# Emptying an attention accumulator at a chunk's end: one ACT copy of its first half, the sum on GpSimd, its second half at the end of the step

## The chip, the cores and the metric

The kernel runs on one core of one Trainium2 chip. The metric is the device time of one execution in microseconds (us). A core has a matrix engine (TensorE: PE, with its weight loads listed as PEld), a vector engine (VectorE, DVE), a scalar engine (ScalarE, ACT), GpSimd (POOL) and SyncE (SP), which here only issues DMAs. Each engine works through its own instructions in order.

## What is computed

```python
scores = (1 / S) * z @ z.T                 # per batch, B = 4, S = 3008, 64 columns of z
attn   = maximum(scores, 0) ** 2
x      = u * (attn @ v)                    # v: 3008 x 256
out    = (sigmoid(x @ w_gate) * (x @ w_val)) @ w_out     # 256 -> 1536 -> 256, 12032 tokens
```

Everything is float32. The kernel keeps precision by splitting operands into a high part and a rest and adding three products.

## The kernel before

**Two stages.** The attention runs for the first half of the time, the gated network (products of 7 per block, L635 to L734) for the second. The change lies in the attention.

**Chunks and steps.** Queries are cut into 6 chunks of 512 (the last 448) per batch, so 24 chunks in all, here numbered 0 to 23. A chunk takes 12 steps, one for each pair of 128-key tiles; `steps` lists all 288, and `k = g % 12` is a step's place in its chunk. Scores are symmetric, so many steps take a tile that an earlier chunk computed, turned and stored in DRAM (`back(s)` is true): they are read back by SP (`load_back`, five steps ahead) and need no scores. Steps of chunk 0 of each batch compute everything, those of chunk 5 nearly nothing.

**One turn of the loop (L854).** For step g the engines get, in this order: PE the scores of step g+2 (`pe_scores`, L354, 6 matmuls); at a chunk's end `keep`; SP the stores of turned tiles; DVE the turning of step g+1 (`turn`, L429 and L433); ACT for step g+2 ReLU and square (`square`, L363 and L364) and rounding to the high part (`round_up`, L379, or DVE's L377); DVE the rest `al` (`rest`, L384); then a list of side work (preparing z, v and the network's weights); last PE the 24 matmuls of step g (`pe_pv`, L507). These are 12 for each half d of the 256 columns of v, and each of the 12 takes 64 of the 128 rows, so that two run side by side into two banks: an accumulator is a pair of banks whose two parts must be added.

**Banks.** PSUM has 8 banks. Banks 0 and 1 take scores. The other six are three pairs that rotate (`pair_of_banks`, L329): `acc_of(b, c, d)` uses pair (2C + d) mod 3 for chunk C. So the new chunk's d = 0 uses the pair that was free, and its d = 1 uses the pair that held d = 0 of the chunk before. The third pair, which held d = 1, takes the scores of every odd step (`scores_of`).

**A chunk's end.** In the loop's turn k = 0 of the next chunk, `keep(..., False)` (L514) does for d = 0 and then d = 1: an ACT copy of one bank to SBUF (L527) and a DVE sum of the other bank to it (L528):

```python
for d in range(NB):
    to, acc = by_half(t[:, d, 0:n]), acc_of(b, c, d)
    nc.scalar.activation(to, product(acc[:, 0, 0:n]), AF.Copy)
    nc.vector.tensor_tensor(to, product(acc[:, 1, 0:n]), to, op=ALU.add)
```

PE's matmuls of d = 1 in that turn write the pair of d = 0 and wait for both. The place `t` lies in the area `keep_a`, two halves in turns; the same area holds tiles that came as stored and are still to be turned (`as_stored`, L455, read by `turn_late`, L482) in batch 0. In the turn k = 1 `keep(..., True)` lets SP store the sums to DRAM (L523). GpSimd only issues DMAs in the attention.

Of the kernel before, what the change touches and what calls it, by code (L numbers as in the profile page):

```python
# [13 lines left out]
AF = mybir.ActivationFunctionType  # L14
ALU = mybir.AluOpType
# [11 lines left out]
def kernel(  # L27
# [10 lines left out]
    nc = tc.nc  # L38
    P = 128
    B, S, D = u.shape  # L40
# [3 lines left out]
    CH = 512  # L44
    NCH = (S + CH - 1) // CH
    NPAIR = (S + 255) // 256
    NB = D // P
# [6 lines left out]
    def chunk(c):  # L54
        return min(CH, S - c * CH)
# [10 lines left out]
    def area(tag, name=None):  # L66
        return pool.tile([P, sizes[tag] * KB], F32, tag=tag, name=name or tag)

    v_a, z_a, zq_a, r_a, ah_a, al_a, al2_a, turned_a, raw_a, zt_a, keep_a, w_a, spare_a = map(area, sizes)
# [3 lines left out]
    def second(tag, name):  # L73

        if tag not in later:
            later[tag] = area(tag, name)
        return later[tag]
# [3 lines left out]
    def part(a, kb, cols, dt=F32):  # L81

        ap = a[:, int(kb * KB) : int(kb * KB) + cols]
        return ap if dt is F32 else ap.bitcast(dt)
# [8 lines left out]
    def product(ap):  # L93

        return ap.rearrange("p (n t) -> p t n", t=2)

    def products(ap):
        return ap.rearrange("p j (n t) -> p j t n", t=2)

    def by_half(ap):  # L100
        return ap.rearrange("p (t n) -> p t n", t=2)

    def by_halves(ap):
        return ap.rearrange("p j (t n) -> p j t n", t=2)
# [19 lines left out]
    def order(b, c):  # L124
        mirrored = [i for i in range(2 * c) if shared(b, i // 2, c)]
        own = [i for i in range(NPAIR) if i not in mirrored]
        last = []
        if halved(b, c):
            own.remove(2 * c + 1)
            last = [2 * c + 1]  # L130
        if not mirrored:
            return own + last
        own.sort(key=lambda i: (i // 2 > c, i // 2 < c and c < NCH - 1, i))
        m = len(own) + len(mirrored)
        places = [x * m // len(own) for x in range(len(own))]
        if (b, c) == (B - 1, NCH - 1):
            places = list(range(len(own)))
        line = [None] * m
        for x, i in zip(places, own):
            line[x] = i  # L140
        rest = iter(mirrored)
        return [next(rest) if i is None else i for i in line] + last

    steps = [(b, c, i) for b in range(B) for c in range(NCH) for i in order(b, c)]
# [96 lines left out]
    def z_place(b, p):  # L241
        n = (b * NCH + p) % 7
        return part(z_a, 2 * n, CH, F32R), part(z_a, 14 + 2 * n, CH, F32R)
# [14 lines left out]
    def turn_z(b, p):  # L258
        z_t[b, p] = part(zt_a, 2 * (p % 2), CH)
        nc.vector.transpose(out=z_t[b, p], in_=z_raw.pop((b, p)))  # L260

    def z_high(b, p):
        nc.scalar.activation(z_place(b, p)[0], z_t[b, p], AF.Copy)  # L263

    def z_low(b, p):
        hi, lo = z_place(b, p)
        nc.vector.tensor_tensor(lo, z_t[b, p], f32(hi), op=ALU.subtract)
# [61 lines left out]
    def pair_of_banks(n):  # L329

        k = 2 + 2 * (n % 3)
        return banks[:, k : k + 2]

    def scores_of(s):

        g = number[s] - 2
        if g % 2:
            return pair_of_banks(2 * (max(g, 0) // NPAIR) + 2)
        return banks[:, 0:2]

# [143 lines left out]
    def acc_of(b, c, d):  # L484

        return pair_of_banks(2 * (b * NCH + c) + d)

    def pe_pv(s):

        b, c, i = s  # L490
        n, k = chunk(c), number[s] % NPAIR
        (ah, al), (vh, vl) = a_of(s), v_place(b, i)
        whole = number[s] >= len(steps) - 2
        for d in range(NB):
            acc = acc_of(b, c, d)
            ds = slice(d * P, (d + 1) * P)
            for j in range(2):
                passes = [(vh, ah), (vl, ah), (vh, al)]
                if i == NPAIR - 1 and j == 1:
                    del passes[1]  # L500
                for x, (vx, ax) in enumerate(passes):
                    start = k == 0 and j == 0 and x == 0
                    ends = j == 1 and x == len(passes) - 1
                    halves = [(0, slice(0, P))] if whole else [(r, rows_half(r)) for r in range(2)]
                    for r, p in halves:
                        stop = ends and number[s] in ((len(steps) - 1, len(steps) - 3)[r], number[s] - k + NPAIR - 1)
                        nc.tensor.matmul(acc[:, r, 0:n], vx[p, j, ds], moving(ax[p, j, 0:n]), start=start, stop=stop)  # L507
                yield
# [2 lines left out]

    sums = dram.tile([P, NB, N], F32, name="sums")

    def keep(b, c, store):  # L514
        n, t0 = chunk(c), b * S + c * CH
        C = b * NCH + c
        if C == B * NCH - 1:
            t = part(turned_a, 8, 2 * CH)
        else:
            t = part(keep_a, 4 * ((C + 1) % 2) if b < B - 1 else 0, 2 * CH)  # L520
        t = t.rearrange("p (h q) -> p h q", h=NB)
        if store:
            nc.sync.dma_start(sums[:, :, t0 : t0 + n], t[:, :, 0:n])  # L523
            return
        for d in range(NB):
            to, acc = by_half(t[:, d, 0:n]), acc_of(b, c, d)
            nc.scalar.activation(to, product(acc[:, 0, 0:n]), AF.Copy)  # L527
            nc.vector.tensor_tensor(to, product(acc[:, 1, 0:n]), to, op=ALU.add)  # L528

# [3 lines left out]
    B1, B2, T12, T34 = range(4)  # L535

    def operand(G, i):

        if G % 2 == 0:
            places = (z_a, 8 * i), (zq_a, 0) if i == T34 else (z_a, 8 * i + 4)  # L540
        else:
            a, o = (v_a, 48 + 8 * i) if i < 2 else (second("r", "x"), 8 * (i - 2))
            places = (a, o), (a, o + 4)
        return [part(a, o, 2 * CH, F32R).rearrange("p (i q) -> p i q", i=2) for a, o in places]
# [201 lines left out]
    with tc.manual_schedule():  # L746
# [5 lines left out]
        def at(when, g, f, *args):  # L752
            when.setdefault(g, []).append((f, args))

        def run(when, g):
            for f, args in when.get(g, ()):
                f(*args)

        per = NPAIR * NCH
        for b in range(1, B):  # L760
            g0 = (b - 1) * per
            for p in range(NCH):
                g = g0 + (3 * NPAIR + 4 * p if p < 3 else 4 * NPAIR + 4 * (p - 3) if p < 5 else 5 * NPAIR)
                if (b, p) == (1, 1):
                    g = 5 * NPAIR + 3
# [7 lines left out]
            for i in range(NPAIR):  # L773
                g = g0 + (2 * NPAIR + 4, 2 * NPAIR + 8, 3 * NPAIR + 2, 3 * NPAIR + 7)[i] if i < 4 else line[i - 4]
# [12 lines left out]
        g = 3 * per  # L787
# [10 lines left out]
        g = len(steps) - NPAIR  # L798
# [55 lines left out]
        for g, (b, c, i) in enumerate(steps[:-2]):  # L854
            nxt = steps[g + 2]
            k = g % NPAIR
            early = g < NPAIR
            if g < 3:
                for _ in pe_pv(steps[g]):
                    pass  # L860
            pe_scores(nxt)
            if early:
                if k + 2 < NPAIR:
                    v_low(0, k + 2)
                if k + 5 < NPAIR:
                    load_v(0, k + 5)
                if k in (2, 3, 5):
                    z_low(0, {2: 3, 3: 4, 5: 5}[k])
                if k in (0, 2, 4):
                    turn_z(0, k // 2 + 3)  # L870
            for s in steps[g + 5 : g + 8]:
                if number[s] - g == (7 if comes_late(s) else 5):
                    load_back(s)
            if k == 0 and g:
                keep(*steps[g - 1][:2], False)
            if k == 1 and g > 1:
                keep(*steps[g - 2][:2], True)
            store_turned(steps[g])
            turn(steps[g + 1])
            if not back(nxt):  # L880
                square(nxt)
            round_up(nxt)
            rest(nxt)
            if g + 4 < len(steps):
                turn_late(steps[g + 4])
            run(before, g)
            if early and k + 3 < NPAIR:
                v_high(0, k + 3)
            if early and k in (1, 2, 4):
                z_high(0, {1: 3, 2: 4, 4: 5}[k])  # L890
            run(after, g)
            if g >= 3:
                for _ in pe_pv(steps[g]):
                    pass
# [5 lines left out]
        extra = {}  # L900
        last = len(groups) * NF - 1
# [16 lines left out]
                    at(extra, (J + NF + (x > 0), (7, 1, 2, 3)[x]), finish, G - 1, t, h)  # L918
        at(extra, (0, -1), load_o, 0)
        at(extra, (0, 1), load_w, 2, 1)  # L920
        at(extra, (0, 7), keep, *steps[-1][:2], False)
        at(extra, (0, 7), keep, *steps[-1][:2], True)
        for F in range(1, NF):
            at(extra, (F - 1, 7), load_o, F)
        for x, F in enumerate((3, 4, 5)):
# [27 lines left out]
        for J in range(last + 1):  # L953
            run(extra, (J, -1))
            for value in range(2):
                k = 4 * value
# [92 lines left out]
```

## Time and profile before

| | |
|---|---|
| median of 3 runs | 1923.06 us (1919.26 to 1923.71) |
| the profiled execution | 1921.55 us, its span 1919.5 us |
| PE busy over the span | 97% |
| DVE, ACT, POOL busy | 81%, 59%, 48% |
| mean granted clock of TensorE | 0.994 |

The span is the time between the first and the last instruction of the profiled execution; 2.05 us lie around it. PE's share is high throughout, so time is won only where PE stands still or runs at a lower clock.

### The profile page before, as it was taken

Reading aid. Unit: us, or ns where it says so; the run is one execution under the profiler, and the core shown is the slowest. Engines: PE = TensorE matmul, PEld = TensorE weight load, DVE = VectorE, ACT = ScalarE, POOL = GpSimd, SP = SyncE. Lnnn points to the kernel's source line nnn. Section 1 sums busy time; section 2 is a strip of 40 time slices with the busy share of each in tenths; the row PEclk is TensorE's granted clock in tenths of the full one; section 3 lists DMA queues with packets and bytes.
Section 4 is the critical chain, followed back from the end, with each engine's and each line's share of the span. In section 5 each row is a group of like instructions: output and inputs, shape, how many; then the busy total and the mean of one; then the engine's idle time right before and its main releaser. Section 6 shows DMA issues by size and latency. Waiting matters only on the chain.

```text
span 1919.5 us, 33838 instructions
## 1 busy us (share of the span) xinstructions
PE 1868.9 (97%) x12614; PEld 1638.3 (85%) x12614; DVE 1563.3 (81%) x2004; ACT 1140.3 (59%) x1520; POOL 921.4 (48%) x853
## 2 busy tenths in 40 slices
PE   9999999999998999999999999999999999999998
PEld 7878988879877888889888888888888888888898
DVE  7887688887888787776888797978888797878886
ACT  8876788767877678765444444444444444534443
POOL 4323200231013200000777777867777777878775
PEclk9999999999999999999999999999999999999999
DMA  7778677986789878886633425242433425242431
GB/s 198 186 197 224 175 177 203 254 262 199 171 220 260 277 174 210 192 234 221 221 92 96 126 69 134 89 102 83 119 100 100 114 69 143 80 102 82 108 100 37
DMA packets 548645, 297.43 MB, mean 155 GB/s; under 512 B 489344, under 2 KB 506176, under 8 KB 548480
## 3 DMA queue, kind: packets, MB, share of 16 engines
q1 hardware_dynamic: 531248, 248.48, 49.2%
q0 software_dynamic: 14832, 46.38, 7.8%
q8 instruction: 99, 1.62, 0.4%
q10 hardware_dynamic: 2400, 0.41, 0.1%
q14 instruction: 66, 0.54, 0.1%
HBM read 192.02 MB, written 103.15 MB: 154 GB/s over the span
## 4 chain that ended last, share of the span: by engine, by line
PE 70%; DVE 2%; ACT 2%; issue 1%; DMA 1%; SPq 0%; DVEq 0%; POOL 0%; POOLq 0%
PE banks L703 18%; PE banks L507 15%; PE banks L643 11%; PE banks L644 11%; PE banks L645 11%; PE banks L354 2%; ACT ah L379 1%; ACT r L363 1%; ACT r L364 1%; PE banks L734 1%; DVE al L384 1%; DMA shared<-turned 1%; DVE keep L528 0%; DVE turned L433 0%; DVE spare L433 0%
## 5 line engine op out<-in xcount | busy, mean ns | idle before, releaser
L507 PE MATMUL banks<-ah,v 64*128 64x512 f32 (+1 forms) x4496 | 748.1, 376 | 39.2 <-DVE keep L528 31.4
L507 PEld LDWEIGHTS banks<-ah,v 64*128 64x128 f32 x4496 | 598.8, 188 | 98.2 <-DVE keep L528 38.8
L507 PE MATMUL banks<-al,v 64*128 64x512 f32 (+1 forms) x2296 | 621.4, 377 | 4.7 <-DVE al L384 3.6
L676 POOL TENSOR_TENSOR keep<-keep,spare 128x512 f32<-128x512 f32 (+1 forms) x284 | 387.3, 1374 | 240.2 <-DVE keep L668 239.1
L384 DVE TENSOR_TENSOR al<-r,ah 128x1024 fp32r<-128x1024 f32 (+1 forms) x287 | 341.2, 1191 | 163.0 <-ACT ah L379 154.9
L507 PEld LDWEIGHTS banks<-al,v 64*128 64x128 f32 x2296 | 387.9, 188 | 37.5 <-DVE al L384 11.0
L379 ACT ACTIVATE ah<-r 128x1024 fp32r<-128x1024 f32 (+1 forms) x252 | 257.5, 1035 | 50.9 <-PE banks L507 28.6
L680 ACT ACTIVATE h<-keep 128x512 fp32r<-128x512 f32 (+1 forms) x144 | 89.7, 623 | 283.7 <-POOL keep L676 280.5
L668 DVE TENSOR_TENSOR zt<-banks,zt 128x512 f32<-128x512 f32 (+1 forms) x288 | 193.8, 673 | 66.7 <-ACT zt L662 59.3
L363 ACT ACTIVATE r<-banks 128x1024 f32<-128x1024 f32 (+2 forms) x169 | 163.5, 967 | 124.4 <-PE banks L354 116.5
L686 POOL TENSOR_TENSOR h<-keep,h 128x512 fp32r<-128x512 f32 (+1 forms) x143 | 186.9, 1307 | 55.7 <-ACT h L680 55.7
L672 ACT ACTIVATE spare<-spare 128x512 f32<-128x512 f32 (+1 forms) x288 | 174.1, 618 | 65.2 <-DVE spare L668 63.6
L668 DVE TENSOR_TENSOR spare<-banks,zt 128x512 f32<-128x512 f32 (+1 forms) x288 | 188.3, 674 | 22.6 <-PE banks L645 22.6
L364 ACT ACTIVATE r<-r 128x1024 f32<-128x1024 f32 (+2 forms) x169 | 169.6, 1003 | 5.4
L662 ACT ACTIVATE zt<-banks 128x512 f32<-128x512 f32 (+1 forms) x144 | 84.0, 583 | 145.7 <-PE banks L645 141.5
L231 POOL DMA_DIRECT2D w_gv<-w x24 | 13.4, 560 | 324.5 <-ACT w L225 311.0
L354 PE MATMUL banks<-z 64*128 64x512 f32 (+2 forms) x1020 | 162.8, 370 | 0.0
L643 PE MATMUL banks<-z,v 128*128 128x512 f32 x378 | 144.1, 381 | 0.0
L645 PE MATMUL banks<-z,v 128*128 128x512 f32 x378 | 143.3, 379 | 0.0
L354 PEld LDWEIGHTS banks<-z 64*128 64x128 f32 x1020 | 126.5, 196 | 10.6 <-ACT z L263 0.8
L680 ACT ACTIVATE v<-keep 128x512 fp32r<-128x512 f32 (+1 forms) x144 | 89.0, 618 | 58.6 <-POOL keep L676 50.5
L668 DVE TENSOR_TENSOR keep<-banks,spare 128x512 f32<-128x512 f32 (+1 forms) x144 | 97.3, 676 | 32.2 <-PE banks L645 28.7
(157 smaller groups left out, 3606.9 us busy)
## 6 DMA issues: line engine op xcount, KB each, us to landing
v<-w_gv SPq DMA_DIRECT2D x75, 896.0 KB, 4.7
r<-shared SPq DMA_DIRECT2D x72, 512.0 KB, 4.6
shared<-turned SPq DMA_DIRECT2D x236, 128.0 KB, 2.8
r<-shared SPq DMA_DIRECT2D x38, 448.0 KB, 5.6
shared<-spare SPq DMA_DIRECT2D x128, 128.0 KB, 3.8
out_dram<-turned SPq DMA_DIRECT2D x176, 64.0 KB, 2.2
w_gv<-w POOLq DMA_DIRECT2D x24, 448.0 KB, 5.0
sums<-keep SPq DMA_DIRECT2D x20, 512.0 KB, 3.7
```

The lines of the kernel that those rows point to most:

```text
L354: nc.tensor.matmul(sc[:, j, 0 : n - q0], keys_of(i, keys[kx], j)[r], queries[qx][r], start=x == 0, stop=x == 2)
L364: nc.scalar.activation(r[:, :, q0:n], r[:, :, q0:n], AF.Square)
L379: nc.scalar.activation(ah[:, :, 0:n], r[:, :, 0:n], AF.Copy)
L384: nc.vector.tensor_tensor(al[:, :, 0:n], r[:, :, 0:n], f32(ah[:, :, 0:n]), op=ALU.subtract)
L507: nc.tensor.matmul(acc[:, r, 0:n], vx[p, j, ds], moving(ax[p, j, 0:n]), start=start, stop=stop)
L643: nc.tensor.matmul(o, wt[:, 0, w], xh, start=True, stop=False)
L644: nc.tensor.matmul(o, wt[:, 0, w], xl, start=False, stop=False)
L645: nc.tensor.matmul(o, wt[:, 1, w], xh, start=False, stop=True)
L668: nc.vector.tensor_tensor(to[:, 0:m], bank(J, value, name), s_t[other][:, 0:m], op=ALU.add)
L676: (nc.vector if J == last else nc.gpsimd).tensor_tensor(y, y, g, op=ALU.mult)
L686: eng.tensor_tensor(lo[:, 0:m], y_t[c][:, 0:m], f32(hi[:, 0:m]), op=ALU.subtract)
L703: nc.tensor.matmul(o, wt[:, half_w, f, ds], moving(ap[:, 0:m]), start=start, stop=stop)
```

## The change

At a chunk's end `free_first` has ACT copy both banks of d = 0 in one instruction of 1024 columns to a place of its own, and GpSimd adds the two parts there. The second half, d = 1, is emptied by `keep(..., 1)` as before with an ACT copy and a DVE sum, but at the end of that turn of the loop, behind `round_up`, `rest` and the side work; its copy writes over the part that GpSimd has read. The place is the area `zq_a`, one for all chunks (the last chunk keeps its own); the network's operand that lay there gets a later tile of that area. `scores_of` gives the scores computed in the turns k = 1 of a chunk banks 0 and 1, since d = 1 is still in its pair then; from k = 3 on odd turns use the pair again. `store_kept` stores in the turn k = 1, as before.

```diff
--- before.py
+++ after.py
@@ -334,7 +334,7 @@
     def scores_of(s):
 
         g = number[s] - 2
-        if g % 2:
+        if g == -1 or g % NPAIR > 2 and g % 2:
             return pair_of_banks(2 * (max(g, 0) // NPAIR) + 2)
         return banks[:, 0:2]
 
@@ -511,21 +511,25 @@
 
     sums = dram.tile([P, NB, N], F32, name="sums")
 
-    def keep(b, c, store):
+    def kept(b, c):
+        last = (b, c) == (B - 1, NCH - 1)
+        t = part(turned_a, 8, 2 * CH) if last else part(zq_a, 0, 2 * CH)
+        return t.rearrange("p (h q) -> p h q", h=NB)[:, :, 0 : chunk(c)]
+
+    def free_first(b, c):
+
+        n, t = chunk(c), kept(b, c)
+        nc.scalar.activation(by_halves(t), products(acc_of(b, c, 0)[:, :, 0:n]), AF.Copy)
+        nc.gpsimd.tensor_tensor(t[:, 0], t[:, 0], t[:, 1], op=ALU.add)
+
+    def keep(b, c, d):
+        to, acc = by_half(kept(b, c)[:, d]), acc_of(b, c, d)[:, :, 0 : chunk(c)]
+        nc.scalar.activation(to, product(acc[:, 0]), AF.Copy)
+        nc.vector.tensor_tensor(to, product(acc[:, 1]), to, op=ALU.add)
+
+    def store_kept(b, c):
         n, t0 = chunk(c), b * S + c * CH
-        C = b * NCH + c
-        if C == B * NCH - 1:
-            t = part(turned_a, 8, 2 * CH)
-        else:
-            t = part(keep_a, 4 * ((C + 1) % 2) if b < B - 1 else 0, 2 * CH)
-        t = t.rearrange("p (h q) -> p h q", h=NB)
-        if store:
-            nc.sync.dma_start(sums[:, :, t0 : t0 + n], t[:, :, 0:n])
-            return
-        for d in range(NB):
-            to, acc = by_half(t[:, d, 0:n]), acc_of(b, c, d)
-            nc.scalar.activation(to, product(acc[:, 0, 0:n]), AF.Copy)
-            nc.vector.tensor_tensor(to, product(acc[:, 1, 0:n]), to, op=ALU.add)
+        nc.sync.dma_start(sums[:, :, t0 : t0 + n], kept(b, c))
 
 
 
@@ -537,7 +541,7 @@
     def operand(G, i):
 
         if G % 2 == 0:
-            places = (z_a, 8 * i), (zq_a, 0) if i == T34 else (z_a, 8 * i + 4)
+            places = (z_a, 8 * i), (second("zq", "low"), 0) if i == T34 else (z_a, 8 * i + 4)
         else:
             a, o = (v_a, 48 + 8 * i) if i < 2 else (second("r", "x"), 8 * (i - 2))
             places = (a, o), (a, o + 4)
@@ -872,9 +876,9 @@
                 if number[s] - g == (7 if comes_late(s) else 5):
                     load_back(s)
             if k == 0 and g:
-                keep(*steps[g - 1][:2], False)
+                free_first(*steps[g - 1][:2])
             if k == 1 and g > 1:
-                keep(*steps[g - 2][:2], True)
+                store_kept(*steps[g - 2][:2])
             store_turned(steps[g])
             turn(steps[g + 1])
             if not back(nxt):
@@ -888,6 +892,8 @@
                 v_high(0, k + 3)
             if early and k in (1, 2, 4):
                 z_high(0, {1: 3, 2: 4, 4: 5}[k])
+            if k == 0 and g:
+                keep(*steps[g - 1][:2], 1)
             run(after, g)
             if g >= 3:
                 for _ in pe_pv(steps[g]):
@@ -918,8 +924,9 @@
                     at(extra, (J + NF + (x > 0), (7, 1, 2, 3)[x]), finish, G - 1, t, h)
         at(extra, (0, -1), load_o, 0)
         at(extra, (0, 1), load_w, 2, 1)
-        at(extra, (0, 7), keep, *steps[-1][:2], False)
-        at(extra, (0, 7), keep, *steps[-1][:2], True)
+        for d in range(NB):
+            at(extra, (0, 7), keep, *steps[-1][:2], d)
+        at(extra, (0, 7), store_kept, *steps[-1][:2])
         for F in range(1, NF):
             at(extra, (F - 1, 7), load_o, F)
         for x, F in enumerate((3, 4, 5)):
```

On ACT at the end of chunk 0, before (L379 rounds, L363 and L364 make the scores' squares, `keep` is the place of the sums):

```order
55 L379 ACTIVATE ah<-r 128x1024
56 L527 ACTIVATE keep<-banks 128x512 x2
57 L363 ACTIVATE r<-banks 128x1024
58 L364 ACTIVATE r<-r 128x1024
59 L379 ACTIVATE ah<-r 128x1024
60 L363 ACTIVATE r<-banks 128x1024
```

The same place with the change (`zq` is the new place, L522 the wide copy):

```order
55 L379 ACTIVATE ah<-r 128x1024
56 L522 ACTIVATE zq<-banks 128x1024
57 L363 ACTIVATE r<-banks 128x1024
58 L364 ACTIVATE r<-r 128x1024
59 L379 ACTIVATE ah<-r 128x1024
60 L527 ACTIVATE zq<-banks 128x512
61 L363 ACTIVATE r<-banks 128x1024
```

Two narrow copies became one wide one in the same place, and a third copy came in behind the rounding of that turn.

On DVE at the same chunk's end, the difference (L433 turns a tile, L384 is the rest `al`):

```order
 L384 TENSOR_TENSOR al<-r,ah 128x1024
-L528 TENSOR_TENSOR keep<-banks,keep 128x512 x2
-L433 STREAM_TRANSPOSE turned<-r 128x16x2x32
-L384 TENSOR_TENSOR al_69<-r,ah 128x1024
+L433 STREAM_TRANSPOSE turned<-r 128x16x2x32
+L384 TENSOR_TENSOR al_69<-r,ah 128x1024
+L528 TENSOR_TENSOR zq<-banks,zq 128x512
 L433 STREAM_TRANSPOSE turned<-r 128x16x2x32
```

The turning and the rest moved ahead of DVE's sum, of which one is left, at the end of the turn.

## Rows read from the trace of the kernel before

**Rows 1.** Busy time of the two stages: PE, PEld, DVE, ACT, POOL, then clock and DMA:
```profile
core 0: us, PE busy (x) PEld busy (x) DVE busy (x) ACT busy (x) POOL busy (x), PEclk, DMA share, GB/s
0.00:915.00 915.00, 869.92 (x7883) 763.21 (x7884) 728.58 (x823) 686.16 (x767) 169.71 (x286) 0.99 0.79 212
915.00:1919.00 1004.00, 998.96 (x4733) 875.11 (x4731) 834.76 (x1182) 454.15 (x755) 751.71 (x568) 1.00 0.38 103
```

**Rows 2.** Who waited for whom in 0 to 915: total us, times, longest:
```profile
PEld banks L507 <- DVE keep L528: 38.8, 22, 3.1
...
PE banks L507 <- DVE keep L528: 31.4, 22, 2.7
...
ACT ah L379 <- DMA r<-shared: 14.8, 8, 3.4
...
PEld banks L507 <- ACT keep L527: 10.0, 8, 4.0
...
PE banks L507 <- ACT keep L527: 7.0, 5, 3.6
```

**Rows 3.** PE at the end of chunk 12, in order of time (start, us, what):
```profile
501.36 0.58 PE L507 MATMUL banks<-al,v 64*128 64x512 f32 x2
501.57 0.39 PE L507 MATMUL banks<-ah,v 64*128 64x512 f32 x1
502.86 0.70 PE L507 MATMUL banks<-ah,v 64*128 64x512 f32 x3 [0.90 <-DVE keep L528]
503.18 0.59 PE L507 MATMUL banks<-al,v 64*128 64x512 f32 x2
```

**Rows 4.** ACT at the end of chunk 12, in order of time:
```profile
500.85 1.06 ACT L527 ACTIVATE keep<-banks 128x512 f32<-128x512 f32 x2
501.81 1.02 ACT L363 ACTIVATE r<-banks 128x1024 f32<-128x1024 f32 x1
502.86 1.06 ACT L364 ACTIVATE r<-r 128x1024 f32<-128x1024 f32 x1
503.95 1.06 ACT L379 ACTIVATE ah<-r 128x1024 fp32r<-128x1024 f32 x1
505.10 1.03 ACT L363 ACTIVATE r<-banks 128x1024 f32<-128x1024 f32 x1
```

**Rows 5.** DVE at the end of chunk 12, in order of time:
```profile
502.12 1.28 DVE L528 TENSOR_TENSOR keep<-banks,keep 128x512 f32<-128x512 f32 x2
503.32 1.50 DVE L433 STREAM_TRANSPOSE spare<-r 128x1024 f32<-128x1024 f32 x1
505.04 1.22 DVE L384 TENSOR_TENSOR al<-r,ah 128x1024 fp32r<-128x1024 f32 x1 [0.22 <-ACT ah L379]
```

**Rows 6.** ACT, DVE and PE at the end of chunk 2:
```profile
131.40 1.09 ACT L527 ACTIVATE keep<-banks 128x512 f32<-128x512 f32 x2 [4.54 <-issue]
...
130.03 1.29 DVE L482 STREAM_TRANSPOSE r<-keep 128x512 f32<-128x512 f32 x2
...
132.05 0.48 PE L507 MATMUL banks<-ah,v 64*128 64x512 f32 x1 [3.65 <-ACT keep L527]
```

**Rows 7.** ACT and PE at the end of chunk 9:
```profile
392.28 0.95 ACT L225 ACTIVATE w<-w 128x896 fp32r<-128x896 f32 x1 [2.00 <-DVE w L221]
393.13 1.06 ACT L527 ACTIVATE keep<-banks 128x512 f32<-128x512 f32 x2
...
392.18 0.38 PE L507 MATMUL banks<-al,v 64*128 64x512 f32 x2
393.76 0.48 PE L507 MATMUL banks<-ah,v 64*128 64x512 f32 x1 [1.21 <-ACT keep L527]
```

**Rows 8.** Busy time and clock: first and last of seven stretches, and one between:
```profile
133.45:136.86 3.41, 3.41 (x20) 2.71 (x18) 1.35 (x3) 3.04 (x3) 0.00 (x0) 0.50 0.41 154
624.97:628.38 3.41, 3.41 (x20) 2.69 (x18) 1.00 (x2) 1.63 (x2) 0.00 (x0) 0.50 1.03 297
505.00:508.41 3.41, 3.41 (x36) 3.01 (x34) 3.27 (x4) 2.99 (x5) 0.00 (x0) 1.00 0.99 256
```

**Rows 9.** GpSimd and DVE in the second stage, in order of time:
```profile
938.74 3.50 POOL L676 TENSOR_TENSOR keep<-keep,spare 128x512 f32<-128x512 f32 x2
942.21 1.28 POOL L686 TENSOR_TENSOR al<-keep,v 128x512 fp32r<-128x512 f32 x1
...
939.26 1.83 DVE L589 TENSOR_TENSOR turned<-turned 128x1024 f32<-128x1024 f32 x1
...
962.28 1.21 DVE L608 TENSOR_TENSOR v<-turned,v 128x1024 fp32r<-128x1024 f32 x1
```

**Rows 10.** SP's queue at the end of chunk 12, and its loads' time to landing:
```profile
503.43 0.56 SPq L523 DMA_DIRECT2D sums<-keep  x1
...
r<-shared SPq DMA_DIRECT2D x72, 512.0 KB, 4.6
```

**Rows 11.** Busy time between the sums of chunks 1 and 2, columns as in the first group:
```profile
91.80:132.30 40.50, 36.10 (x332) 31.46 (x332) 36.91 (x47) 29.74 (x33) 14.13 (x24) 1.00 0.82 211
```

## The prediction

> **What bounds the kernel now.** I read the busy time of the two stages first. In the attention PE is busy 869.92 of 915 us, in the network 998.96 of 1004 [rows 1]. The change touches only the attention, so its reach is the 45 us in which PE stands there, and whatever PE loses at a lower clock. The table of waits says what those 45 us are: PE waited 31.4 us for DVE's sum at a chunk's end and 7.0 us for ACT's copy there [rows 2]. Nearly all of PE's idle time lies at the 23 changes of chunk. The weight loads show the same waits with 38.8 and 10.0 us [rows 2]; they are longer because the end of a matmul is modelled, and its tail covers part of the wait. Which is nearer is seen at one change. A pair of matmuls starts 0.21 us after the pair before (501.36, 501.57). At the end of chunk 12 the next pair should run at 501.57 and the one with `al` at 502.00; it ran at 503.18 [rows 3]. So 1.18 us were lost where PE's row says 0.90. The true sum lies between 38.4 and 48.8, near the upper end; I take 47 us, two a change.
>
> Then the clock. The granted clock is 1.00 nearly everywhere, but in seven stretches of 3.41 us it is 0.50 (1.2 instead of 2.4 GHz), the first at 133.45 and the last at 624.97 [rows 8]. All seven begin at a chunk's end, five up to 1.3 us behind PE's wait there and two just before it ended, and only at changes that cost PE 1.9 us or more, though not at all of these. In such a stretch 20 matmuls started, at full clock 36 [rows 8]: 16 times 0.095 us, 1.5 us each, 10.6 us for seven. So the waits and what follows them cost some 58 us.
>
> **The change, part by part.**
>
> *The wait of PE's second half.* Before, both banks of d = 0 come free with DVE's first sum, which stands behind ACT's copy and behind whatever DVE has in hand. Now they come free with one ACT copy of 1024 columns. The trace has that shape from PSUM to SBUF: ReLU took 1.02 us [rows 4]; I take 1.03, and 0.06 from there to PE. At chunk 12's end ACT begins at 500.85 [rows 4], so PE may go on at 501.94, and wanted to at 501.57 [rows 3]: 0.37 us are left of 1.18. I did this for each of the 23 changes (copy's start plus 1.09, less the time when PE came). In nine ACT begins so early that nothing is left. In nine, like chunk 12's, 0.2 to 0.6 us are left, together 3.5. In four (ends of chunks 8, 9, 13 and 15) ACT itself is late: at chunk 9's end the copy begins at 393.13, behind a 0.95 us piece of weight work, and PE came at 392.40, one pair after 392.18 [rows 7]; 1.8 us stay. The four keep 5.8 together. Left: 9 us. The 23rd is the next part.
>
> *The place.* At chunk 2's end ACT waited 4.54 us until 131.40 [rows 6]. What ended just then is DVE's turning out of `keep_a` (130.03 plus 1.29) [rows 6], the area that the copy writes. PE lost 3.65 us to it, and more behind it. The new place is not shared with those tiles, so this wait goes whole; it is in the 47.
>
> *ACT's extra work.* It reads 512 columns more a change: 1.03 for the wide copy and 0.58 for the late one against 1.06 for two [rows 4], 0.55 us. The first ReLU behind the copy begins as before (1.03 against 1.06). The late copy sits ahead of the next ReLU. At chunk 12's end: copy to 501.88, ReLU, square, rounding to about 505.0, late copy to 505.6, ReLU to 506.6, where it ended at 506.13 before [rows 4].
>
> *Scores in one pair of banks.* In the turns k = 0, 1 and 2 the scores now share banks 0 and 1, so PE's scores wait for the ReLU of the turn before. At chunk 12's end PE, going on at 501.94, needs 1.29 us for d = 1, 0.65 for scores and 2.58 for the next 24 matmuls (all by 0.215 a pair): it wants the banks again at 506.46, and gets them at 506.6. That is 0.2 us, in the four changes into a chunk 1; in the others a step that is read back lies between, or DVE does the rounding, and the ReLU is earlier. 1 us in all.
>
> *DVE.* It loses one sum of 0.64 us a change, and turning and rest come 1.28 us earlier [rows 5]. A gain without effect where DVE isn't late, and a help to `al` behind the change.
>
> *GpSimd.* 23 sums. Its like, two SBUF inputs of 512 columns, takes 1.28 us alone; two in a row beside a DVE operation with two SBUF inputs took 3.50, so the slower one 2.3, and that DVE operation 1.83 where its like took 1.21 without [rows 9]. The rest `al` is such an operation [rows 5]. Bounds for DVE are 0 and 0.62 a change (14 us); I take 2 us on PE's path, as DVE was often turning then. ACT's late copy must wait for GpSimd: done 1.3 to 2.3 us behind the wide copy, while ACT has 3.1 us of ReLU, square and rounding [rows 4]. Only where the next step is read back is there 1.06 us of cover; the up to 1.2 us then falls on an ACT that has no squares to make.
> The Trainium skill, "SBUF — State Buffer", section "Who interferes with whom", speaks against this part: a VectorE instruction with two SBUF inputs and a GpSimd instruction that reads SBUF exclude each other for the whole instruction. The rows above agree with it. By it the rest could stand behind a whole GpSimd sum of 1.28 us, 29 us over 23 changes, and the time would be about 1911 if PE saw it all; by the rows' 0.62 it is 14.
>
> *SP.* The store of the sums is issued in the same turn, but DVE's last sum now stands behind the rest: 506.9 instead of 503.40, so SP, which issued at 503.43 [rows 10], is held up to 3.5 us. Behind it are stores and the reads of stored tiles. These are issued five steps ahead and used by ACT three turns later, 9.7 us by 0.215 a pair, and land in 4.6 [rows 10]: 5.1 us of cover against 3.5. But ACT already waited eight times for such a tile, 14.8 us in all [rows 2], mostly unseen by PE.
>
> *What is late next.* PE now reaches the following steps 2 us earlier, and the stalls were also when others caught up. DVE was busy 36.91 of 40.50 us before chunk 2's end [rows 11]; ACT's eight waits for tiles come 2 us closer to PE. I take 5 us for this, bounds 0 and 20.
>
> *The clock.* If long waits bring the low stretches, five of seven go with waits that fall under 1.9 us, and chunks 9 and 15, left with 1.8, may keep theirs: 7.6 us, bounds 0 and 10.6.
>
> **The sum**, against the profiled execution (1921.55, which is 1.5 under the runs' median): −47 + 9 + 1 + 2 + 5 − 7.6 = −37.6, so **1884 us**. With the better bounds (−48.8 + 9 − 10.6) 1871; with 38.4 for the waits and 20 given back and no clock 1912.
>
> **The rivals.**
>
> *The stall moves on* (15%). Behind each change PE waits for `al` or for a tile instead, and half returns: 1884 + 19 = 1903. For it: DVE with 3.6 us to spare where 5 are to be won [rows 11], and the waits for tiles. Against it: those waits hardly reached PE, and DVE's work falls.
>
> *The two engines on one door* (8%). GpSimd's sum stretches the rest by 0.62 us at every change and PE sees it: 14 us instead of the 2 in the sum, 1896. Against it: DVE is turning, with one input, for 1.5 us of each such step [rows 5].
>
> *SP is held, and tiles come late* (4%). This is the case of a slower kernel. Place: the store of sums in SP's queue, 3.5 us later [rows 10], with reads behind it. It decides once a tile takes over 6.2 us to land, and outweighs the gain from 37.6/23 = 1.6 us of PE a change on. With 2.5 us it gives 1884 + 57 = 1941.
>
> *Nothing changes* (3%). The single place makes ACT's copy wait for the store before, as the shared area did at chunk 2's end, and the waits stay: about 1921. Against it: that store was issued 11 steps earlier and lands in a few us.
>
> **How the numbers follow.** The forecast as summed has 70%, its own range 1873 to 1895. With most of the first two rivals 1872 to 1903 holds eight in ten. A measurement tells 0.3% (6 us) from no change. Faster by more: forecast and first two rivals, 93%; within it 3%; slower 4%.
>
> **What would show it.** Right: PE's wait for DVE's sum gone, a wait of 0.3 us for the wide copy in its place and some 1.8 at the ends of chunks 9 and 15; the wide copy at 1.03 us; ACT's 4.54 us at chunk 2's end gone; five or more low stretches gone; the network's stage as long as before, starting some 37 us earlier. Wrong: ACT waiting for GpSimd by more than a microsecond in steps with squares, PE waiting for ReLU before scores, DVE's rest at 1.8 us behind changes, or ACT's wait for tiles well over 15 us.

## The result and the profile after

The changed kernel took 1890.5 us (median of four runs, 1889.5 to 1894.8), before 1922.5: a ratio of 0.984, interval 0.982 to 0.986. It is faster by 32 us. Forecast were 1884 and a gain of 38; the range, 1872 to 1903, holds the time.

The profiled execution here took 1894.8 us, the slowest of its four. So the same kernel was measured a second time; sums are made on the profile of that measurement (1890.4 us), which I call the repeat.

> The changed kernel once more, unaltered, beside the next one on the same chip: 1889 to 1892.

1891.7 us, ratio 0.985 (0.984 to 0.987).

Busy times of the page, PE, DVE, ACT and POOL:

```profile
PE 1859.8 (98%) x12614; PEld 1622.3 (86%) x12614; DVE 1562.2 (83%) x1981; ACT 1148.9 (61%) x1520; POOL 954.6 (50%) x876
```

The two stages, columns as in [rows 1]:

```profile
0.00:886.00 886.00, 858.96 (x7874) 745.29 (x7875) 725.89 (x797) 693.37 (x764) 200.90 (x307) 1.00 0.82 218
886.00:1892.00 1006.00, 1000.89 (x4742) 877.03 (x4740) 836.27 (x1185) 455.53 (x757) 753.73 (x570) 1.00 0.38 103
```

The attention ends 27 us earlier in this execution (32 in the repeat), and the network behind it takes as long as before. PE still stands 27 us of the 886, where it stood 45 of 915 [rows 1]. The table of waits of the changed kernel, in the attention, says on whom:

```profile
PEld banks L507 <- DVE al L384: 33.0, 53, 1.3
...
ACT ah L379 <- DMA r<-shared: 25.0, 11, 3.9
...
PE banks L507 <- DVE al L384: 14.7, 28, 0.9
...
ACT v L293 <- DMA raw<-in_v_dram: 13.6, 5, 4.7
...
PEld banks L507 <- ACT zq L522: 12.5, 14, 2.0
...
PE banks L507 <- ACT zq L522: 6.9, 10, 1.6
...
ACT zq L527 <- POOL zq L523: 4.4, 8, 0.7
```

The wait for DVE's sum [rows 2] is gone. In its place stand a short one for the wide copy (L522) and a longer one for the rest `al`. Before, the waits for `al` and for v were these:

```profile
PEld banks L507 <- DVE al L384: 11.0, 20, 1.3
...
PE banks L507 <- DVE al L384: 3.6, 8, 0.9
...
ACT v L293 <- DMA raw<-in_v_dram: 3.1, 2, 1.6
```

The end of chunk 12, which answers to [rows 3, 4 and 5], on PE, ACT and POOL:

```profile
485.60 0.38 PE L507 MATMUL banks<-al,v 64*128 64x512 f32 x2
485.95 0.70 PE L507 MATMUL banks<-ah,v 64*128 64x512 f32 x4
...
484.89 1.01 ACT L522 ACTIVATE zq<-banks 128x1024 f32<-128x1024 f32 x1
485.79 1.03 ACT L363 ACTIVATE r<-banks 128x1024 f32<-128x1024 f32 x1
486.85 1.06 ACT L364 ACTIVATE r<-r 128x1024 f32<-128x1024 f32 x1
487.94 1.06 ACT L379 ACTIVATE ah<-r 128x1024 fp32r<-128x1024 f32 x1
488.91 0.58 ACT L527 ACTIVATE zq<-banks 128x512 f32<-128x512 f32 x1
...
485.99 1.40 POOL L523 TENSOR_TENSOR zq<-zq 128x512 f32<-128x512 f32 x1 [36.17 <-ACT zq L522]
```

This is the step as it was worked out: the wide copy in 1.01 us, PE going on 0.05 behind it, 0.35 between two pairs where 0.21 is usual and 1.29 stood before. GpSimd's sum lies under ACT's squares.

**The bill by terms.** I took the time between the starts of neighbouring matmuls of the attention, less 0.215 us (0.43 in low-clock stretches), from 20 us on, by what ended the wait (us; waits of less than 60 ns left out; the last four columns are runs of the next section):

```
                       before   repeat   without sum  write only  loads first  sum on DVE
DVE's sum / ACT's copy   43.8      8.2          9.5         8.3         10.6         8.4
al and ah                 5.3     19.4         11.9        12.5         14.9        14.0
low-clock stretches         7        0            0           0            0           0
```

The waits at the changes fell by 35.6 us (forecast 38), the clock gave back seven stretches, 10.6 at the prediction's 1.5 us each (forecast 7.6), and `al` with `ah` took 14.0 by the unrounded sums (forecast 8 for all that comes back). That makes 32.2; between the two profiled executions lie 31.2. Ahead of 20 us both profiled executions of the changed kernel have one low stretch that the kernel before had not, at 11.8 and 10.9 us; at the end of the first chunk the two are 0.5 and 0.1 us behind the kernel before, so it cost little.

### The profile page after: what moved, and what is told of

Same layout as the page of the kernel before. It is cut to its first block, busy times and chain, and to the rows that moved or that the text cites. A ratio compares the mean times of both kernels' runs of the same rounds, so it can differ in the third digit from the quotient of the medians.

```text
span 1893.0 us, 33807 instructions
## 1 busy us (share of the span) xinstructions
PE 1859.8 (98%) x12614; PEld 1622.3 (86%) x12614; DVE 1562.2 (83%) x1981; ACT 1148.9 (61%) x1520; POOL 954.6 (50%) x876
## 4 chain that ended last, share of the span: by engine, by line
PE 79%; ACT 6%; DVE 6%; issue 4%; DMA 4%; POOL 1%; SPq 1%; DVEq 0%; POOLq 0%; ACTq 0%
PE banks L507 22%; PE banks L707 19%; PE banks L647 12%; PE banks L648 11%; PE banks L649 11%; PE banks L354 3%; DVE al L384 2%; ACT ah L379 2%; ACT r L364 1%; ACT r L363 1%; DMA r<-shared 1%; SPq L410 1%; PE banks L738 1%; DMA shared<-turned 1%; DVE turned L433 1%
## 5 line engine op out<-in xcount | busy, mean ns | idle before, releaser
L507 PE MATMUL banks<-ah,v 64*128 64x512 f32 (+1 forms) x4496 | 668.6, 373 | 10.4 <-ACT zq L522 6.9
L507 PEld LDWEIGHTS banks<-ah,v 64*128 64x128 f32 x4496 | 424.4, 186 | 65.0 <-ACT zq L522 12.5
L507 PE MATMUL banks<-al,v 64*128 64x512 f32 (+1 forms) x2296 | 438.3, 377 | 15.4 <-DVE al L384 14.7
L384 DVE TENSOR_TENSOR al<-r,ah 128x1024 fp32r<-128x1024 f32 (+1 forms) x287 | 345.1, 1205 | 126.9 <-ACT ah L379 122.7
L379 ACT ACTIVATE ah<-r 128x1024 fp32r<-128x1024 f32 (+1 forms) x252 | 257.0, 1033 | 56.0 <-DMA r<-shared 25.0
L507 PEld LDWEIGHTS banks<-al,v 64*128 64x128 f32 x2296 | 218.4, 186 | 59.2 <-DVE al L384 33.0
L523 POOL TENSOR_TENSOR zq<-zq 128x512 f32<-128x512 f32 (+1 forms) x23 | 34.7, 1508 | 352.4 <-ACT zq L522 208.0
L363 ACT ACTIVATE r<-banks 128x1024 f32<-128x1024 f32 (+2 forms) x169 | 163.2, 965 | 69.5 <-PE banks L354 64.2
L364 ACT ACTIVATE r<-r 128x1024 f32<-128x1024 f32 (+2 forms) x169 | 170.3, 1008 | 5.5
L354 PE MATMUL banks<-z 64*128 64x512 f32 (+2 forms) x1020 | 131.5, 364 | 0.1
L672 DVE TENSOR_TENSOR spare<-banks,spare 128x512 f32<-128x512 f32 (+1 forms) x144 | 97.1, 674 | 26.0 <-PE banks L649 22.3
```

The source lines that it names most:

```text
L354: nc.tensor.matmul(sc[:, j, 0 : n - q0], keys_of(i, keys[kx], j)[r], queries[qx][r], start=x == 0, stop=x == 2)
L364: nc.scalar.activation(r[:, :, q0:n], r[:, :, q0:n], AF.Square)
L379: nc.scalar.activation(ah[:, :, 0:n], r[:, :, 0:n], AF.Copy)
L384: nc.vector.tensor_tensor(al[:, :, 0:n], r[:, :, 0:n], f32(ah[:, :, 0:n]), op=ALU.subtract)
L672: nc.vector.tensor_tensor(to[:, 0:m], bank(J, value, name), s_t[other][:, 0:m], op=ALU.add)
```

## The experiments

Three theories for the 14 us, and what each run had to tell: theory 1, DVE is late with its own work now that PE comes earlier; theory 2, GpSimd's sum costs, by the prediction's "door", that is by holding DVE's operations up (2a), or by what stands behind it in GpSimd's queue (2b); theory 3, SP is held by the store.

**The place alone** on the kernel before:

```diff
-            t = part(keep_a, 4 * ((C + 1) % 2) if b < B - 1 else 0, 2 * CH)
+            t = part(zq_a, 0, 2 * CH)
...
-            places = (z_a, 8 * i), (zq_a, 0) if i == T34 else (z_a, 8 * i + 4)
+            places = (z_a, 8 * i), (second("zq", "low"), 0) if i == T34 else (z_a, 8 * i + 4)
```

> The kernel before with one edit: the sums of a chunk go to the area zq_a instead of keep_a. If the shared area cost what the trace of before showed at chunk 2's end (3.65 us of PE, its tail of 0.2, and one low-clock stretch of 1.5 us), this alone wins 4 to 6 us: about 1917. PE's wait for DVE's sum stays at 30 us or more. If the wait at chunk 2's end was DVE's backlog and not the place, the wait moves on to DVE's sum there and nothing is won: 1922.

1920.6 us, ratio 1.000 (0.999 to 1.001): nothing. The end of chunk 2 on ACT, DVE and PE:

```profile
127.28 1.06 ACT L527 ACTIVATE zq<-banks 128x512 f32<-128x512 f32 x2
...
132.78 1.28 DVE L528 TENSOR_TENSOR zq<-banks,zq 128x512 f32<-128x512 f32 x2
...
133.51 1.22 PE L507 MATMUL banks<-ah,v 64*128 64x512 f32 x3 [4.39 <-DVE zq L528]
```

ACT's copy now begins at 127.28 instead of 131.40 [rows 6], as wanted, but DVE, still busy with its other work, reaches its sums only at 132.78, and PE waits on for them: 4.39 us. The named wait was ACT's, the time was DVE's. In the changed kernel, where DVE no longer stands between the bank and PE, it is gone. Six low-clock stretches were still there, one of them twice as long as the others.

**Without GpSimd's sum**, the line with `nc.gpsimd.tensor_tensor` taken out:

> The changed kernel without GpSimd's 23 sums, so the second part of d = 0 is missing in the output. Theory 1 (the new waits for the rest al are DVE's backlog, now that PE comes earlier): time unchanged within 2 us, waits for al stay near 20 us by starts of matmuls, as GpSimd held DVE up for only some 4 us in all. Theory 2 (GpSimd's sum holds DVE on the shared door, ACT's late copy, and the loads queued behind it): al waits fall to 8 us or less and the time falls by 8 to 12 us.

1881.3 us, ratio 0.979 (0.977 to 0.981). So the 23 sums cost 9 us, where I had put 2. `al` and `ah` fell to 11.9 in the table above, by 7.5. Theory 2, then, but not yet by which way.

**The store later:**

```diff
-            if k == 1 and g > 1:
-                store_kept(*steps[g - 2][:2])
+            if k == 3 and g > 3:
+                store_kept(*steps[g - 4][:2])
```

> The changed kernel with the store of the sums issued in the turn k = 3 instead of k = 1, when DVE's last sum is long done and SP needn't wait for it. Theory 3 (SP is held there and reads of stored tiles land late): ACT's waits for read-back tiles fall from 25 to 15 us or less and the time falls by 4 to 8 us. Theory 1 and 2: time unchanged within 2 us, as PE hardly waits for those tiles.

1887.0 us, ratio 0.982 (0.980 to 0.984); its interval overlaps with that of the changed kernel (0.982 to 0.986) and barely misses that of the repeat (0.984 to 0.987). So the gain of some 3.5 us is hardly clear of noise. ACT's waits for read-back tiles were 21.3 us (25.0 in the first profile, 22.4 in the repeat), not 15. If it wins anything, it is not by the way that theory 3 names.

**Less work on DVE**, the weight pieces' `low_words` and `add` left out:

```diff
-        jobs = ("load", "abs", "shift", "sign", "low_words", "add", "sums", "parts", "store")
+        jobs = ("load", "abs", "shift", "sign", "skip", "skip", "sums", "parts", "store")
```

> The changed kernel without three of VectorE's side operations in each of the 18 weight pieces (low words and their sum, about 1.7 us a piece, 31 us in all): the weights lose their low words. Theory 1: DVE's backlog sets the waits for al, so they fall from 20 us to 10 or less, and the time falls by 8 to 12 us to about 1880. Theory 2 and 3: al waits stay over 16 us and the time falls by less than 4.

1879.8 us, ratio 0.978 (0.976 to 0.980). `al` alone fell to 9.1 us by starts. As theory 1 says, PE waits where DVE is late; 34 us less of DVE's busy time on the page gave 11. The waits that went here, 9.3 us with `ah`, and the 7.5 that went without the sum are more than 14 together, so in part they are the same waits. The same cut was not made in the kernel before, so how much of the 11 belongs to the change is not shown.

**GpSimd writes only**, and then **writes three times**:

```diff
-        nc.gpsimd.tensor_tensor(t[:, 0], t[:, 0], t[:, 1], op=ALU.add)
+        nc.gpsimd.memset(t[:, 0], 0.0)
```

> The changed kernel with GpSimd's sum replaced by a GpSimd instruction that fills the same 512 columns with zeros: it still waits for ACT's wide copy and holds its queue, but reads nothing from SBUF, and it is shorter; the first half of the sums is lost in the output. Theory 2a (the shared door: GpSimd's reading stretches DVE's rest): the rest stays at 1.22 us everywhere and the time falls to that without the sum, 1881 to 1883. Theory 2b (the queue: loads of z and v stand behind an instruction that waits for ACT, so they start later): ACT's wait for v stays near 13 us and the time at 1887 to 1890.

1882.8 us, ratio 0.980 (0.978 to 0.982). That is the time that 2a forecast. But the fill takes only 0.53 us, so the queue behind it moves on sooner too. Hence the longer one:

> The kernel with GpSimd filling zeros instead of summing, three times over, so that GpSimd is busy some 1.5 us at a change, as long as with the sum; the first half of the sums is lost. Theory 2a (what costs is that GpSimd reads SBUF and DVE's operations stand behind it): 1881 to 1884, DVE's rest at 1.22 us throughout. If GpSimd's length costs instead (ACT's late copy waits for it): 1887 to 1891.

1890.1 us, ratio 0.984 (0.983 to 0.985): the whole 9 us are back, with nothing read. DVE was not stretched. The rest's group and that of a weight operation (L187), in the stretch 0 to 915, first of the repeat, then of the long write:

```profile
L384 DVE TENSOR_TENSOR al<-r,ah 128x1024 fp32r<-128x1024 f32 (+1 forms) x287 | 344.9, 1205 | 122.7 <-ACT ah L379 113.1 <-PE banks L354 4.9 <-DMA shared<-spare 0.4
...
L187 DVE TENSOR_SCALAR w<-w 128x512 f32<-128x512 f32 x18 | 10.7, 595 | 0.0
```

```profile
L384 DVE TENSOR_TENSOR al<-r,ah 128x1024 fp32r<-128x1024 f32 (+1 forms) x287 | 340.5, 1189 | 129.3 <-ACT ah L379 118.0 <-PE banks L354 4.9 <-PE banks L507 1.5
...
L187 DVE TENSOR_SCALAR w<-w 128x512 f32<-128x512 f32 x18 | 7.8, 434 | 0.0
```

The sum cost DVE 4.4 and 2.9 us in these groups, 10.6 over the whole page (1562.8 against 1552.2); without that stretch the time is the same within 2 us. Theory 2a falls as the main cost. The other price of a long GpSimd instruction that was expected, ACT's late copy waiting for it, falls too: in the long write that copy waits for GpSimd nowhere, in the repeat nine times, 4.6 us in all. GpSimd's queue, theory 2b, is left.

**The loads first**, with the store at k = 3:

```diff
-        nc.gpsimd.tensor_tensor(t[:, 0], t[:, 0], t[:, 1], op=ALU.add)
+
+    def add_first(b, c):
+        t = kept(b, c)
+        nc.gpsimd.tensor_tensor(t[:, 0], t[:, 0], t[:, 1], op=ALU.add)
...
-            if k == 0 and g:
-                keep(*steps[g - 1][:2], 1)
+            if k == 1 and g > 1:
+                keep(*steps[g - 2][:2], 1)
             run(after, g)
+            if k == 0 and g:
+                add_first(*steps[g - 1][:2])
```

> The changed kernel with the store at k = 3, GpSimd's sum moved behind the loads of the turn k = 0 in its queue, and the second half d = 1 emptied at the end of the turn k = 1, since its copy must come behind the sum. Compared with the later store alone (1887). Theory 2b: ACT's wait for v falls from 14 to 5 us or less and the time to 1881 to 1884. Theory 2a: the rest is stretched as before and the time stays at 1886 to 1888.

1886.3 us, ratio 0.981 (0.979 to 0.984), no better than the later store alone: by the time alone that is the answer of 2a. ACT's wait for v did fall to 4.5 us, as 2b has it. Where the time went shows when the runs are laid side by side: how much later than in the write-only kernel the rest of the sixth step of a chunk ended (us, counted by L384's instructions):

```
middle of chunk     4     6  |   10    12  |   16    18  |   23
repeat            0.2   3.9  |  3.6   6.9  |  6.0   8.5  |  9.1
later store       0.8   1.8  |  1.5   6.6  |  6.7   7.6  |  6.1
loads first       1.4   1.9  |  2.8   3.2  |  6.3   5.9  |  6.9
write long        0.4   3.1  |  3.5   5.7  |  7.7   8.6  |  8.5
```

The repeat loses 3.7, 3.3 and 2.5 us around chunks 5, 11 and 17: all of its 9. Those are the chunks in which z and v of the next batch are loaded, by GpSimd's queue. With the loads ahead of the sum these three losses are 0.5, 0.4 and −0.4. Its pair is the later store alone, with 1.0, 5.1 and 0.9; the 5.1 hold a low-clock stretch, at 425.96, worth some 1.7. So with the loads first the loss in these chunks is gone, but two thirds of it at chunks 5 and 17 went with the later store already, with the loads issued as late as before. What a late load costs hangs on more than its place in the queue. The version with the loads first gave as much away elsewhere: against the write-only kernel PE waited 2.2 us by starts for DVE's last sum, which this version had put a step later, 2.3 more for the wide copy (2.0 of them at one change) and 2.4 more for `al`. Why is open.

How a late load reaches PE is seen on DVE behind the end of chunk 4: its turning of z, in the repeat, with the later store, and with the sum on DVE (below):

```profile
207.04 0.71 DVE L260 STREAM_TRANSPOSE zt<-raw 128x512 f32<-128x512 f32 x1 [3.29 <-DMA raw<-in_z_dram]
```

```profile
204.81 0.71 DVE L260 STREAM_TRANSPOSE zt<-raw 128x512 f32<-128x512 f32 x1 [0.47 <-DMA raw<-in_z_dram]
```

```profile
204.85 0.70 DVE L260 STREAM_TRANSPOSE zt<-raw 128x512 f32<-128x512 f32 x1
```

In the repeat DVE stands 3.29 us for z, the rests behind it come late, and PE waits 0.8 us by starts for `al` at 209.4. In the other two PE has no such wait in this chunk.

The end of chunk 10 on POOL and ACT (the repeat also on PE), in the kernel before, then in the repeat, with the loads first, and with the single fill:

```profile
420.82 0.66 POOL L253 DMA_DIRECT2D raw<-in_z_dram  x1
...
428.29 0.60 ACT L527 ACTIVATE keep<-banks 128x512 f32<-128x512 f32 x1
```

```profile
412.52 1.02 ACT L522 ACTIVATE zq<-banks 128x1024 f32<-128x1024 f32 x1
...
413.68 1.35 POOL L523 TENSOR_TENSOR zq<-zq 128x512 f32<-128x512 f32 x1 [8.62 <-issue]
414.98 0.66 POOL L253 DMA_DIRECT2D raw<-in_z_dram  x1
...
425.87 0.63 ACT L293 ACTIVATE v<-raw 128x512 fp32r<-128x512 f32 x1 [4.49 <-DMA raw<-in_v_dram]
...
426.95 0.46 PE L507 MATMUL banks<-al,v 64*128 64x448 f32 x2 [0.88 <-DVE al L384]
```

```profile
408.90 0.59 POOL L284 DMA_DIRECT2D raw<-in_v_dram  x1
...
412.17 1.01 ACT L522 ACTIVATE zq<-banks 128x1024 f32<-128x1024 f32 x1
```

```profile
408.88 1.02 ACT L522 ACTIVATE zq<-banks 128x1024 f32<-128x1024 f32 x1
...
410.52 0.66 POOL L253 DMA_DIRECT2D raw<-in_z_dram  x1
```

Before, GpSimd ran ahead and issued z's first load 7.5 us ahead of ACT's copy. Now it stands idle for 8.6 us in front of its sum, and the load comes 2.5 us behind the copy's start. ACT then waits 4.5 us for v, and PE for `al`. With the loads first v's load is out 3.3 us ahead of the copy. The single fill also waits for the copy, and its load comes 1.6 us behind the copy's start; that kernel lost only 1.5 us against the one without the sum. So the wait for ACT alone is not what costs 9 us here, but the wait and the sum's length together: the loads had room for the one and not for both.

**The sum on DVE:**

```diff
-        nc.gpsimd.tensor_tensor(t[:, 0], t[:, 0], t[:, 1], op=ALU.add)
+
+    def add_first(b, c):
+        t = kept(b, c)
+        nc.vector.tensor_tensor(t[:, 0], t[:, 0], t[:, 1], op=ALU.add)
...
                 free_first(*steps[g - 1][:2])
+                add_first(*steps[g - 1][:2])
```

> The changed kernel with the sum of d = 0 on DVE, at the head of the turn k = 0, instead of GpSimd: 0.65 us more of DVE at each of 23 changes, none on GpSimd. Theory 2: most of the 9 us that GpSimd's sum cost come back, 1883 to 1886, as DVE gains 4 us that the door cost and loses 15 us that lie mostly beside other work. Theory 1 (DVE's backlog is what PE waits for): DVE's extra work goes to PE, 1890 or more.

1882.4 us, ratio 0.980 (0.978 to 0.982). The sum comes right behind ACT's copy, at the head of the turn. Its 15 us of DVE cost no more than the 1 us by which this run is slower than the one without the sum, and GpSimd's queue is free again: theory 1 had expected DVE's extra work to go to PE (1890 or more), and it did not.

**The copy late**, made three times over:

```diff
+        for _ in range(3):
             nc.scalar.activation(by_halves(t), products(acc_of(b, c, 0)[:, :, 0:n]), AF.Copy)
```

> The changed kernel with the wide copy made three times over, so that PE's second half waits some 2.06 us more at a change. If it is PE's wait that brings the low clock, stretches at 0.50 come back, three or more, where the wait passes 1.9 us, and the time is 1890 plus 30 to 45 us, 1920 to 1935. If the low clock of the kernel before had another cause (the sums' place, DVE's order), no or one stretch comes back and only the waits add.

1943.1 us, ratio 1.012 (1.009 to 1.014). That is more than the 1920 to 1935 expected. PE waited 48.4 us by starts for the copy, 40 more, and eleven low-clock stretches came back. First two stretches of 3.41 us, the first of the eleven and the one behind it, columns as in [rows 8]:

```profile
96.70:100.11 3.41, 3.41 (x20) 2.71 (x18) 2.12 (x2) 1.47 (x3) 3.41 (x6) 0.50 0.46 121
...
100.30:103.71 3.41, 3.41 (x36) 3.01 (x34) 1.19 (x2) 3.35 (x5) 3.21 (x6) 1.00 1.04 334
```

Ten of the eleven begin within 2 us of the end of such a wait (1.7 to 3.9 us); the one at 690.7 begins 0.9 us behind a wait of 2.5 us for `ah`. Other changes with waits of 1.4 to 2.4 us had none. So the waits bring the low clock, and their length alone does not tell which one will.

**Three together**, then **two**: sum on DVE, store at k = 3, and, in the first only, two weight pieces begun one step later:

```diff
-        starts = [24, 31, *range(84, 127, 7), *range(156, 199, 7), 246, 261]
+        starts = [24, 31, 84, 91, 98, 105, 113, 119, 126, 156, 163, 170, 177, 185, 191, 198, 246, 261]
```

> The changed kernel with the sum of d = 0 on DVE, the store at k = 3, and two of the 18 weight pieces begun one step later, so that their ACT copy no longer stands ahead of the wide copy at the ends of chunks 9 and 15. The three act on different waits: 8 us (GpSimd), 3.5 us (SP) and twice 1.8 us: 1875 to 1879. If they overlap, as PE's next wait is DVE's backlog in each case, 1880 to 1882.

1892.0 us, ratio 0.985 (0.984 to 0.987), no better than the change. ACT, DVE and PE behind the end of chunk 9:

```profile
386.80 0.88 ACT L182 ACTIVATE w<-w 128x512 f32<-128x512 f32 x1 [2.39 <-DVE w L226]
...
385.68 1.08 DVE L226 TENSOR_TENSOR w<-w 128x896 fp32r<-128x896 f32 x1
...
391.31 0.70 PE L507 MATMUL banks<-ah,v 64*128 64x512 f32 x4 [3.65 <-ACT ah L379]
```

The moved piece ends in the turn in which the next begins. ACT's first operation of the next piece waits 2.39 us for DVE's last of this one, in front of the squares, and PE stands 3.65 us. Two low-clock stretches came back with it.

> The changed kernel with the sum of d = 0 on DVE and the store at k = 3, the weight pieces where they were. If the moved weight pieces spoiled the three together (1892), these two add up: 1878 to 1881. If the two don't go together (with the later store DVE's sum and the reads of stored tiles fall otherwise), 1886 to 1892.

1883.5 us, ratio 0.981 (0.980 to 0.982). That lies between the two times expected. So the moved pieces did spoil the three, by 8.5 us; and the later store adds nothing to the sum on DVE. The best version found is the changed kernel with its sum on DVE, 1882.4 us, 8 under the change as it was.

## Why the prediction was right, and where it was off

- **What bounds the kernel: right.** The changes of chunk were the time to be won, and the wait for DVE's sum went whole. Its size, 47, was about right: 43.8 by starts over all 23, which leaves out some 0.1 us a wait by which the next pair still came late (rows 3 have it in the 1.18).
- **The wait that stays: right.** Forecast 9 us, measured 8.2, with 1.6 at chunk 9's end as PE's row has it (1.8 by starts). The four changes where ACT was forecast to be late took 5.6 (forecast 5.8). At chunk 9's end GpSimd and DVE met too:

```profile
380.83 1.01 ACT L522 ACTIVATE zq<-banks 128x1024 f32<-128x1024 f32 x1
...
381.89 0.70 PE L507 MATMUL banks<-ah,v 64*128 64x512 f32 x4 [1.64 <-ACT zq L522]
...
381.98 1.86 POOL L523 TENSOR_TENSOR zq<-zq 128x512 f32<-128x512 f32 x1 [10.69 <-issue]
...
381.61 1.07 DVE L226 TENSOR_TENSOR w<-w 128x896 fp32r<-128x896 f32 x1
382.81 2.11 DVE L384 TENSOR_TENSOR al<-r,ah 128x1024 fp32r<-128x1024 f32 x1
```

- **The shared door: the mechanism right, its cost on the path small.** The rest took 2.11 us beside GpSimd's sum (1.22 in [rows 5]), and the sum 1.86 beside DVE's L226, which is what the Trainium skill, "SBUF — State Buffer", section "Who interferes with whom", says: with two SBUF inputs against a GpSimd instruction that reads SBUF, one waits for the other. But PE didn't wait for this `al`: the step had room. At single changes the stretch passed the bound of 0.62 (it was up to 1.1), but in the repeat only seven rests were stretched. Over all changes the rest lost 4.4 us, and the long write, without the stretch, was no faster by more than 2. The 29 us of the rule with PE seeing it all are far off.
- **GpSimd's term, 2 us: the step that failed.** I costed its sum by the door and by ACT's late copy, and left out what is queued behind it on GpSimd. (The slower of the two sums in [rows 9] took 2.2 us by the rows, not 2.3; nothing hangs on that.) The sum waits for ACT, and the loads of z and v, which ran ahead before, wait with it and then for the sum itself. It cost 9 us in three chunks. That is shown by the runs without a sum on GpSimd, by the long write, which reads nothing and costs the same, and by the loads put first, which take the loss out of these chunks though not out of the total.
- **"What is late next", 5 us:** the kind was right (`al`, DVE's backlog, shown by the run with less DVE work). Without GpSimd's sum 11.9 us of these waits are left, 6.6 more than before.
- **The clock: right in kind, cautious in number.** All seven stretches went, not five: 10.6 us for 7.6 at the forecast's price. That price was a little low: 20 and 36 in [rows 8] count every matmul that ran in a stretch, also those begun ahead of it; by starts 16 fell into the first stretch and 32 into the one at full clock, so a stretch cost about 1.7 us and the seven some 12. With that the bill above comes to 33.5 against 31.2. The clock hid 3 us or more of what GpSimd's term lacked, and that was luck.
- **The place: wrong as its own gain.** "This wait goes whole" held only together with the release by ACT alone; the new place by itself gave nothing.
- **Scores in one pair of banks: 1 us**, not seen: by starts PE has no wait of 60 ns or more that a ReLU ended.
- **The rivals.** "The stall moves on" came in part, for a reason that it didn't name. The sign named for SP did show: ACT's waits for tiles grew from 14.8 to 22 or 25 us. But PE's waits for `ah` came to only 1.4 us by starts in the repeat, nothing like 1.6 us a change, and the sum on DVE has 25.2 us of such waits in ACT and is 8 us faster. So late tiles are not what cost the time.

## What to carry to other kernels

When work moves to an engine that so far only issued DMAs, its first waiting instruction ends that engine's running ahead: list the loads behind it in its queue, and the room that each has, before the arithmetic is costed. A wait named in a profile is worth its time only if nothing else ends just behind it; here the place was free 4 us earlier and PE gained nothing. Fixes that each win alone should be run together before they are summed: one of 8.1 us and one of 3.5 (hardly clear of noise) gave 7.0 together.

## What the runs showed of the hardware

- GpSimd's sum also held up a DVE operation with one SBUF input and constants (L187): in the repeat the three of its 18 that ran beside a sum took 1.51 us, the other fifteen 0.37 to 0.44. The mean, 595 ns against 414 before, hides that.
- The granted clock fell to 0.50 for 3.41 us behind PE's waits of 1.7 to 3.9 us for the copy that was made three times, in ten cases, and not behind others of up to 2.4. In the attention of the changed kernel, where the longest wait at a change was 1.8, it fell only once, at 10.9 and 11.8 us of the two profiled executions, before the first chunk was done.
